# Attention and two feed-forward layers in float32: the first 24 attention steps and the first block of both layers as whole float32 products, and the weights split after that block has used them

## The chip, the cores and the metric

The kernel runs on one core of one Trainium2 chip. The core has a matrix engine (TensorE, "PE" in the profile, with its weight loads shown apart as "PEld"), three engines that work on vectors (VectorE "DVE", ScalarE "ACT", GpSimd "POOL"), and SyncE ("SP"), from which this kernel issues all its DMAs. The engines run side by side, each through its own instructions in order, and wait for each other through semaphores. The metric is the device time of one execution in microseconds, lower is better.

## The reference

```python
# 8 batches, 8 heads, 512 local and 32 global tokens, head size 64; float32
s_g = scale * np.matmul(q_g, k_all.transpose(0, 1, 3, 2))
out_g = np.matmul(sm(s_g), v_all)                  # 32 global queries see all 544 keys
s_ll = np.where(np.abs(pos[:, None] - pos[None, :]) <= 32, s_ll, -1e9)
a_l = sm(np.concatenate([s_lg, s_ll], axis=-1))    # a local query: the 32 global keys and a window of 65
out_l = np.matmul(a_l, np.concatenate([v_g, v_l], axis=2))
...
x = attn_out.transpose(0, 2, 1, 3).reshape(4352, 512)
h = x @ w_in                                       # 512 x 2048
g = h * (1.0 / (1.0 + np.exp(-h)))
return (g @ w_out).astype(np.float32)              # 2048 x 512
```

The weights come as float64; the kernel turns them into float32 on the chip.

## The kernel before

**Products of split operands.** PE takes operands of the type float32r, which hold fewer bits than float32. To keep float32 accuracy, nearly every operand is split: ACT writes a rounded copy "hi" (a CAST), and DVE or POOL writes the rest "lo" as a difference. One wanted product is then three on PE: hi by hi, hi by lo, lo by hi. So the queries and keys of a step become qk and klo (`st_split`, L339/L340 for the first 28 steps, L342 to L344 later), the values vhi and vlo (L350/L351), the transposed probabilities pt_hi and pt_lo (L396/L397, and for the columns of the global queries L404/L405), the attention output xh and xl (L427/L428), the activations gh and gl (L559/L560), and the weights w_hi and w_lo (L238/L239).

**Attention in steps.** A step is a chunk of 128 local queries for a pair of heads; there are 128 steps, 16 to a batch. Step k loads its queries and keys (`st_load`), splits them, forms the scores (`st_scores`, L369: 6 products of 224 columns), runs the softmax on DVE and ACT (L373 to L382), and copies the probabilities by a DMA from SBUF to SBUF into a float32r tile rr (L385), since the transposes take float32r. `st_turn` transposes four 128x128 blocks on PE (L393) and splits the result; `st_out` multiplies by the values (L421: 12 products of 128 or 160 columns, for 64 output rows) and writes 128 rows of the layers' input. The global queries of a batch go the same way in four pairs of heads: `g_load`, `g_split` (L253 to L255), `g_scores` (L268 to L270: 6 products of 272 columns), `g_soft`, `g_move` (two DMAs to float32r tiles rg), `g_turn` (10 transposes a batch, L310/L313).

**Weights.** `load_weights` brings in one piece of a slice: 512 columns (256 towards the end) of 128 rows as pairs of 32-bit words. ACT scales the upper words (L231), three integer operations of DVE put the float32 together (L233, L234, L236), ACT casts w_hi (L238) and POOL subtracts w_lo (L239). There are 16 slices f, each with 512 columns of the first layer's weights and 512 of the second's.

**The two layers in blocks.** The token tiles (128 rows each) are taken in 12 blocks of three or two (`SIZES`). For each block and each slice f, `first_layer` issues 12 products of 384 columns (L550), the activation follows (tanh on ACT L556, DVE L557, then the split), and `second_layer` of the slice before issues 9 products of 512 columns (L569 to L571).

**Order.** PE's program order is the order in which the Python code emits it; the other engines' instructions are put in order by a scheduler at build time. The attention is a list of pieces with due times (`DUE`, `LAG`, `HEADS`), and `advance` emits those that are due. Before block 0 the code emits steps 0 to 11, which feed block 0's three token tiles; during block n the call `fill` emits the steps that block n+1 needs, so steps 12 to 23 run beside block 0. During block 0 each slice also asks for the weights three slices ahead (`LOOK`). Buffers that only the first steps use live in two pools (`first_pool`) that are closed once they are empty and whose room then holds the last four slices of weights.

Of the kernel before, what the change touches and what calls it, by code (L numbers as in the profile page):

```python
# [33 lines left out]
NEG = -8.0e9              # times the scale of 1/8: -1e9  # L34
SCALE = 0.125

# [1 line left out]
SIZES = [3, 2] + [3] * 9 + [2]       # token tiles in each block of the two layers  # L38
NLATE = 4                            # slices of the weights that take the place of the first buffers
# [19 lines left out]
PRE, PACE, LOOK = 0, 0.75, 1         # weights converted during the first steps  # L59
END = 0.6                            # how far the attention is ahead of a block  # L60
# [13 lines left out]
CLOSE = 9  # L74
# [16 lines left out]
ND = 28  # L91

@with_exitstack
def attention_moe_kernel(ctx: ExitStack, tc: tile.TileContext, qk0_in, qk_in, v_in, gqk, wts, out):
# [7 lines left out]
    # buffers of the first steps, in two parts that later hold the last slices of the weights  # L102
# [6 lines left out]
    # until the layers start, attention has their banks too  # L109
# [33 lines left out]
    # probabilities: columns past the window stay zero  # L143
    probs = []
    for i in range(BUFS["p"]):
        t = const.tile([P, 2, 2 * P], F32, name=f"probs{i}")
# [5 lines left out]
    held = [set() for _ in first]  # L152
    pts = []
    for home in (const, first_pool[0])[: 1 + (PTS > 0)]:
        pts.append([home.tile([P, 2, 2, P + SG], F32R, name=f"pt_{part}{len(pts)}") for part in ("hi", "lo")])
        for t in pts[-1]:
            nc.gpsimd.memset(t.bitcast(F32), 0.0)
    if PTS:
        held[0].add(f"pt{PTS - 1}")

    def pt_tiles(k):
        return pts[k % 2 if k < PTS else 0]
# [4 lines left out]
    closing, turns, uses = [], itertools.count(), itertools.count()  # L167
# [5 lines left out]
    def raw_tile(name):  # L173
        if first[0] and not closing and next(uses) % 3 == 0:
            held[0].add(name)
            return first_pool[0].tile([P, QW + KW], F32, tag="raw", name=name)
        return raws.tile([P, QW + KW], F32, tag="raw", name=name)

    def qk_tiles(name):
        if first[0] and not closing and next(turns) % 3 == 0:  # L180
            held[0].add(name)
            pool, bufs = first_pool[0], (1, 1)
        else:
            pool, bufs = work, BUFS["qk"]
        return (pool.tile([P, QW + KW], F32R, tag="qk", bufs=bufs[0], name=f"qk{name}"),
                pool.tile([P, SKV], F32R, tag="klo", bufs=bufs[1], name=f"klo{name}"))

    def rr_tile(k):
        if k % 2 and k < RRS and first[0]:
            held[0].add(f"rr{k}")  # L190
            return first_pool[0].tile([P, 4 * P], F32R, tag="rr", bufs=1, name=f"rr{k}")
        return work.tile([P, 4 * P], F32R, tag="rr", bufs=BUFS["rr"], name=f"rr{k}")
# [4 lines left out]
    w_hi, w_lo, w_next = [], [], [0, 0]  # L197

    def load_weights():
        f, c0 = w_next  # L200
        i = (f - (NF - NLATE)) // 2
        if f == CLOSE and not closing:
            closing.append(f)
        if i >= 0 and first[i]:
# [5 lines left out]
            first_pool[i] = ctx.enter_context(tc.tile_pool(name=f"late{i}", bufs=1, side=side, reuse_waits="tile"))  # L210
        if c0 == 0:
            home = const if i < 0 else first_pool[i]
            w_hi.append(home.tile([P, 2 * DM], F32R, name=f"w_hi{f}"))
            w_lo.append(home.tile([P, 2 * DM], F32R, name=f"w_lo{f}"))
# [13 lines left out]
        # float64 to float32: the upper word read as float32 and scaled by 2**-112 has the exponent  # L228
# [439 lines left out]
```

## Time and profile before

| what | value |
|---|---|
| time, median of 3 runs (lowest, highest) | 1109.2 us (1108.95, 1109.77) |
| span of the profiled execution | 1108.1 us |
| time of a run beyond that span, by the median | 1.1 us |
| first product of the first layer, block 0 | 86.37 us |
| first product of the first layer, block 1 | 206.58 us |
| bytes moved by DMA | 134.76 MB, of them 86.44 MB read from HBM |

Times inside the execution count from the start of its span. "Busy" is the time in which an engine has an instruction in work; on PE successive products overlap, so what one product costs is read from the distance between the starts of two neighbours, not from its duration. The row PEclk gives the share of full speed at which TensorE's clock was granted. A form such as `128x384 f32` is partitions by elements.

### The profile page before, as it was taken

The page shows a single profiled execution, that of the slowest core. Times are in us where ns is not written, and L with a number is a line of the kernel's source. Part 1 is how long each engine was busy: PE and PEld are TensorE (multiplying, and loading weights), DVE is VectorE, ACT ScalarE, POOL GpSimd, SP SyncE. Part 2 cuts the span into 40 slices and gives each one's busy share as a digit, 9 for nine tenths or more (in the row PEclk, how much of TensorE's full clock was granted, in tenths as well). Part 3 has the DMA queues.
Part 4 walks back from the last instruction along what each step waited for, and adds up shares of the span by engine and source line. Part 5 has one row for each costly group of instructions (what it writes and reads, how often), then busy time and mean ns, then how long its engine had stood idle before and what let it go on. Part 6 is the DMA issues. An engine that isn't in the chain of part 4 may idle for free.

```text
span 1108.1 us, 21579 instructions
## 1 busy us (share of the span) xinstructions
PE 1042.5 (94%) x6824; PEld 947.8 (86%) x6824; DVE 798.5 (72%) x2467; ACT 725.1 (65%) x1933; POOL 228.5 (21%) x441
## 2 busy tenths in 40 slices
PE   5647889999999999999999999999999999999998
PEld 4646778898999999999989999999999999889996
DVE  6989998777778867766667877777777768863322
ACT  7876676776677766766567776667666658763232
POOL 8756775321100111001010111101100011100000
PEclk8678899999999999999999999999999999999999
DMA  8576554543343443342233443334333324420000
GB/s 249 179 219 188 182 170 130 156 121 117 109 145 115 138 138 110 113 148 83 82 112 112 147 130 117 111 116 158 109 109 120 111 92 148 138 76 20 1 30 19
DMA packets 74800, 134.76 MB, mean 122 GB/s; under 512 B 10432, under 2 KB 30400, under 8 KB 74688
## 3 DMA queue, kind: packets, MB, share of 16 engines
q1 hardware_dynamic: 74688, 133.40, 38.8%
q8 instruction: 54, 0.88, 0.3%
q14 instruction: 58, 0.48, 0.1%
HBM read 86.44 MB, written 8.91 MB: 86 GB/s over the span
## 4 chain that ended last, share of the span: by engine, by line
PE 80%; DVE 10%; DMA 3%; issue 3%; ACT 3%; POOL 1%; SPq 0%; DVEq 0%; ACTq 0%; POOLq 0%
PE h L550 31%; PE out L569 11%; PE out L571 10%; PE out L570 10%; PE o L421 8%; PE s L369 4%; PE t L393 3%; DVE w L234 2%; DVE w L236 1%; DMA rr<-probs 1%; DMA raw_w<-in_wts_dram 1%; DVE raw_w L233 1%; DVE pt_lo L397 1%; ACT probs L377 1%; DVE probs L373 1%
## 5 line engine op out<-in xcount | busy, mean ns | idle before, releaser
L550 PE MATMUL h<-xh,w_hi 128*128 128x384 f32 (+1 forms) x768 | 255.6, 333 | 0.1
L550 PE MATMUL h<-xh,w_lo 128*128 128x384 f32 (+1 forms) x768 | 252.3, 329 | 0.0
L550 PE MATMUL h<-xl,w_hi 128*128 128x384 f32 (+1 forms) x768 | 252.1, 328 | 0.0
L569 PE MATMUL out<-w_hi,gh 128*128 128x512 f32 x544 | 224.8, 413 | 0.0
L571 PE MATMUL out<-w_hi,gl 128*128 128x512 f32 x544 | 215.6, 396 | 3.0 <-DVE gl L560 1.8
L570 PE MATMUL out<-w_lo,gh 128*128 128x512 f32 x544 | 214.7, 395 | 0.0
L556 ACT ACTIVATE t<-h 128x384 f32<-128x384 f32 (+1 forms) x192 | 90.5, 471 | 186.2 <-PE h L550 175.8
L404 POOL CAST pt_hi<-pgt 128x64 fp32r<-128x64 f32 (+1 forms) x160 | 50.4, 327 | 726.1 <-PE o L421 719.2
L557 DVE SCALAR_TENSOR_TENSOR t<-t,h 128x384 f32<-128x384 f32 (+1 forms) x192 | 101.6, 529 | 122.7 <-ACT t L556 121.7
L550 PEld LDWEIGHTS h<-xh,w_hi 128*128 128x128 f32 x768 | 145.4, 189 | 6.0 <-ACT xh L427 0.6
L550 PEld LDWEIGHTS h<-xl,w_hi 128*128 128x128 f32 x768 | 145.5, 189 | 5.4
L550 PEld LDWEIGHTS h<-xh,w_lo 128*128 128x128 f32 x768 | 145.3, 189 | 0.0
L560 DVE TENSOR_TENSOR gl<-t,gh 128x384 fp32r<-128x384 f32 (+1 forms) x192 | 107.3, 559 | 48.5 <-PE out L571 43.1
L571 PEld LDWEIGHTS out<-w_hi,gl 128*128 128x128 f32 x544 | 102.8, 189 | 28.4 <-DVE gl L560 4.6
L377 ACT ACTIVATE probs<-probs,st 128x224 f32<-128x224 f32 x256 | 121.4, 475 | 7.3 <-DVE st L373 6.2
L373 DVE CUSTOM_DVE_ANT_0 probs<-s,mask 128x224 f32<-128x224 f32 x256 | 89.3, 384 | 50.4 <-PE s L369 47.0
L421 PE MATMUL o<-pt_hi,vhi 128*64 128x160 f32 (+1 forms) x512 | 99.4, 238 | 20.1 <-ACT pt_hi L396 7.8
L570 PEld LDWEIGHTS out<-w_lo,gh 128*128 128x128 f32 x544 | 103.6, 190 | 11.2
L569 PEld LDWEIGHTS out<-w_hi,gh 128*128 128x128 f32 x544 | 103.2, 190 | 11.4 <-ACT gh L559 0.4
L559 ACT CAST gh<-t 128x384 fp32r<-128x384 f32 (+1 forms) x192 | 94.6, 493 | 21.2 <-DVE t L557 17.8
L421 PE MATMUL o<-pt_hi,vlo 128*64 128x160 f32 (+1 forms) x512 | 96.3, 237 | 0.0
L421 PE MATMUL o<-pt_lo,vhi 128*64 128x160 f32 (+1 forms) x512 | 79.8, 238 | 16.3 <-DVE pt_lo L397 11.8
(82 smaller groups left out, 2016.5 us busy)
## 6 DMA issues: line engine op xcount, KB each, us to landing
raw<-in_qk_dram SPq DMA_DIRECT2D x100, 352.0 KB, 3.0
rr<-probs SPq DMA_DIRECT2D x128, 256.0 KB, 2.3
vraw<-in_v_dram SPq DMA_DIRECT2D x128, 128.0 KB, 2.4
raw_w<-in_wts_dram SPq DMA_DIRECT2D x28, 512.0 KB, 4.0
raw_g<-in_gqk_dram SPq DMA_DIRECT2D x32, 304.0 KB, 2.8
out_dram<-o SPq DMA_DIRECT2D x32, 256.0 KB, 2.6
raw<-in_qk_dram SPq DMA_DIRECT2D x28, 240.0 KB, 3.6
rg<-pg SPq DMA_DIRECT2D x16, 256.0 KB, 2.4
```

The lines of the kernel that those rows point to most:

```text
L373: nc.vector.tensor_tensor_reduce(out=p[:, u, :W], in0=s[:, u * W : (u + 1) * W], in1=mask_of[c], scale=-SCALE, scalar=3.0e38, op0=ALU.add, ...
L377: nc.scalar.activation(p[:, u, :W], p[:, u, :W], AF.Exp, bias=st[:, u : u + 1], scale=-1.0, accum_out=st[:, 2 + u : 3 + u])
L404: nc.gpsimd.tensor_copy(out=pt_hi[:n, :, a, P:], in_=g)
L421: nc.tensor.matmul(o[:D, u * wide : u * wide + m], v[:, a, u, :], pt[:, u, a, :m], start=(i == 0), stop=(i == len(terms) - 1))
L550: nc.tensor.matmul(h[:, :nt], wt, x[:, c, :nt], start=(i == 0), stop=(i == 3 * NCC - 1))
L556: nc.scalar.activation(t[:, :nt], h[:, :nt], AF.Tanh, scale=0.5)
L557: nc.vector.scalar_tensor_tensor(out=t[:, :nt], in0=t[:, :nt], scalar=1.0, in1=h[:, :nt], op0=ALU.add, op1=ALU.mult)
L559: nc.scalar.copy(out=gh[:, :nt], in_=t[:, :nt])
L560: nc.vector.tensor_tensor(out=gl[:, :nt], in0=t[:, :nt], in1=gh[:, :nt].bitcast(F32), op=ALU.subtract)
L569: nc.tensor.matmul(o, gh[:, sl], wh, start=(f == 0), stop=False)
L570: nc.tensor.matmul(o, gh[:, sl], wl, start=False, stop=False)
L571: nc.tensor.matmul(o, gl[:, sl], wh, start=False, stop=(f == NF - 1))
```

## The change

- For the first 24 steps (`KF`) and the global queries of the first two batches (`GF`) nothing is split. Scores, transposes and value products take the float32 tiles as they were loaded: a product is one instruction with float32 operands where three with float32r stood. The copies rr and rg are not made for them; the transposes read the probabilities themselves.
- Block 0's input, activations and weights stay float32 too: 4 products instead of 12 in `first_layer`, 3 instead of 9 in `second_layer`. Half of the copies of block 0's input move from ACT to DVE; its xl and gl are not made.
- `load_weights` makes only the float32 weights, with two DVE operations instead of three; ACT's scaling uses the function Prelu with a slope instead of Copy. `split_weights(f)`, called behind block 0's `second_layer` of slice f, makes w_hi on ACT and w_lo on POOL for the later blocks. The float32 slice f lies where w_lo of slice f+1 will lie, and the last one lies in the buffer of block 0's xl.
- Buffers: five tiles of probabilities instead of two in the first 12 steps, up to six for the loaded queries and keys, two single tiles for transposed probabilities where one hi/lo pair stood. The first weight pools are closed one slice earlier, and `CLOSE` goes from 9 to 8.

```diff
+KF = 24
+GF = 2
-CLOSE = 9
+CLOSE = 8
...
-        nc.scalar.activation(w, words[:, :, 1].bitcast(F32), AF.Copy, scale=2.0**-112)
-        wi, up, low = w.bitcast(U32), words[:, :, 1].bitcast(U32), words[:, :, 0].bitcast(U32)
-        nc.vector.tensor_scalar(out=up, in0=wi, scalar1=3, scalar2=None, op0=ALU.logical_shift_left)
-        nc.vector.scalar_tensor_tensor(out=wi, in0=wi, scalar=0x80000000, in1=up, op0=ALU.bitwise_and,
+        nc.scalar.activation(w, words[:, :, 1].bitcast(F32), AF.Prelu, scale=2.0**-112, alpha=-(2.0**32))
+        wi, low = w.bitcast(U32), words[:, :, 0].bitcast(U32)
+        nc.vector.tensor_scalar(out=low, in0=low, scalar1=29, scalar2=None, op0=ALU.logical_shift_right)
+        nc.vector.scalar_tensor_tensor(out=wi, in0=wi, scalar=3, in1=low, op0=ALU.logical_shift_left,
                                        op1=ALU.bitwise_or)
-        nc.vector.scalar_tensor_tensor(out=wi, in0=low, scalar=29, in1=wi, op0=ALU.logical_shift_right,
-                                       op1=ALU.bitwise_or)
-        nc.scalar.copy(out=hi, in_=w)
-        lows(2 * f + c0 // DM < POOLW).tensor_tensor(out=lo, in0=w, in1=hi.bitcast(F32), op=ALU.subtract)
+    def split_weights(f):
+        w_hi.append(slot(f, late, F32R, "wh", f"w_hi{f}"))
+        w_lo.append(slot(f, late, F32R, "ws", f"w_lo{f}"))
+        for c0 in range(0, 2 * DM, DM):
+            sl = slice(c0, c0 + DM)
+            hi, lo, w = w_hi[f][:, sl], w_lo[f][:, sl], w_32[f][:, sl]
+            nc.scalar.copy(out=hi, in_=w)
+            nc.gpsimd.tensor_tensor(out=lo, in0=w, in1=hi.bitcast(F32), op=ALU.subtract)
...
     def st_scores(k, b, c, pr):
-            if k < ND:
+            if k < KF:
+                terms = [(raw[:, qs], raw[:, QW : QW + W])]
+            elif k < ND:
...
     def st_turn(k, b, c, pr):
+            if whole:
+                nc.tensor.transpose(t[:, i * P : (i + 1) * P], p[:, i * P : (i + 1) * P], ident.bitcast(F32))
+                continue
             nc.tensor.transpose(t[:, i * P : (i + 1) * P].bitcast(F32R), rr[:, i * P : (i + 1) * P], ident)
...
     def st_out(k, b, c, pr, t):
+            if whole:
+                terms = [(vraw, pt_f, a) for a in range(2)]
...
-            nc.scalar.copy(out=xh[rows, pr, sl], in_=src)
-            nc.vector.tensor_tensor(out=xl[rows, pr, sl], in0=src, in1=xh[rows, pr, sl].bitcast(F32),
-                                    op=ALU.subtract)
+            if n == 0 and u == 0:
+                nc.scalar.copy(out=xh[rows, pr, sl], in_=src)
+            elif n == 0:
+                nc.vector.tensor_copy(out=xh[rows, pr, sl], in_=src)
...
     def first_layer(n, f):
+            if n == 0:
+                nc.tensor.matmul(h[:, :nt], w_32[f][:, c * P : (c + 1) * P], xh[:, c, :nt], start=(c == 0),
+                                 stop=(c == NCC - 1))
+                continue
...
     def second_layer(n, f, gh, gl):
+            if n == 0:
+                nc.tensor.matmul(o, gh[:, sl], wh, start=(f == 0), stop=(f == NF - 1))
...
+        if n == 0:
+            split_weights(f)
```

More of the change, by code (lines that the diff above doesn't have):

```diff
@@ L91 @@
 ND = 28
+KF = 24
+GF = 2
+RRS = 12
 @with_exitstack
@@ L144, in attention_moe_kernel @@
     probs = []
-    for i in range(BUFS["p"]):
-        t = const.tile([P, 2, 2 * P], F32, name=f"probs{i}")
+    for i in range(BUFS["p"] + 3):
+        home = const if i < BUFS["p"] else first_pool[0]
+        t = home.tile([P, 2, 2 * P], F32, name=f"probs{i}")
         nc.gpsimd.memset(t, 0.0)
@@ L152, in attention_moe_kernel, with pt_whole, probs_tile @@
     held = [set() for _ in first]
+    held[0].update(f"p{k}" for k in range(RRS) if k % len(probs) >= BUFS["p"])
     pts = []
[L154 to L159, printed above, removed]
-    def pt_tiles(k):
-        return pts[k % 2 if k < PTS else 0]
+    def pt_tiles(k):
+        if not pts:
+            for part in ("hi", "lo"):
+                pts.append(work.tile([P, 2, 2, P + SG], F32R, tag=f"pt_{part}", name=f"pt_{part}"))
+                nc.gpsimd.memset(pts[-1].bitcast(F32), 0.0)
+        return pts
+    def pt_whole(k):
+        return work.tile([P, 2, 2, P + SG], F32, tag="pt_lo" if k % 2 else "pt_hi", name=f"pt{k}")
+    def probs_tile(k):
+        i = k % (len(probs) if k < RRS else BUFS["p"])
+        held_by[i] = k
+        return probs[i]
+    held_by = {}
     acc = const.tile([P, NPR, P], F32, name="acc")
-    closing, turns, uses = [], itertools.count(), itertools.count()
+    closing, homes = [], itertools.count()
     def free(name):
@@ L171, in free, with raw_tile @@
             names.discard(name)
-    def raw_tile(name):
-        if first[0] and not closing and next(uses) % 3 == 0:
+    def raw_tile(name, whole=False):
+        i = next(homes) % (2 if closing else 3) if whole else 0
+        if i == 2:
             held[0].add(name)
-            return first_pool[0].tile([P, QW + KW], F32, tag="raw", name=name)
+            return first_pool[0].tile([P, QW + KW], F32, tag="raw", bufs=2, name=name)
+        if i == 1:
+            return work.tile([P, QW + KW], F32, tag="qk", bufs=BUFS["qk"][0], name=name)
         return raws.tile([P, QW + KW], F32, tag="raw", name=name)
     def qk_tiles(name):
[L180 to L186, printed above, removed]
+        return (work.tile([P, QW + KW], F32R, tag="qk", bufs=BUFS["qk"][0], name=f"qk{name}"),
+                work.tile([P, SKV], F32R, tag="klo", bufs=BUFS["qk"][1], name=f"klo{name}"))
     def rr_tile(k):
-        if k % 2 and k < RRS and first[0]:
-            held[0].add(f"rr{k}")
-            return first_pool[0].tile([P, 4 * P], F32R, tag="rr", bufs=1, name=f"rr{k}")
         return work.tile([P, 4 * P], F32R, tag="rr", bufs=BUFS["rr"], name=f"rr{k}")
@@ L195, in lows, with slot @@
         return nc.gpsimd if pool else nc.vector
-    w_hi, w_lo, w_next = [], [], [0, 0]
+    w_32, w_hi, w_lo, w_next = [], [], [], [0, 0]
+    def slot(i, late, dtype, tag, name):
+        home = const if i < NF - NLATE else first_pool[(i - (NF - NLATE)) // 2]
+        assert i < NF - NLATE or late[(i - (NF - NLATE)) // 2]
+        return home.tile([P, 2 * DM], dtype, tag=f"{tag}{i}", name=name)
+    late = [False, False]
     def load_weights():
         f, c0 = w_next
-        i = (f - (NF - NLATE)) // 2
+        i = (f + 1 - (NF - NLATE)) // 2
         if f == CLOSE and not closing:
             closing.append(f)
-        if i >= 0 and first[i]:
+        if 0 <= i < 2 and first[i]:
             while held[i]:
@@ L327, in st_vload @@
     def st_vload(k, b, c, pr):
-        vraw = raws.tile([P, 2, 2, D], F32, tag="vraw", bufs=BUFS["vraw"], name=f"vraw{k}")
+        if k < KF and k % 2:
+            vraw = two.tile([P, 2, 2, D], F32, tag="vhi" if k % 4 == 1 else "vlo", name=f"vraw{k}")
+        else:
+            vraw = raws.tile([P, 2, 2, D], F32, tag="vraw", bufs=BUFS["vraw"], name=f"vraw{k}")
         nc.sync.dma_start(out=vraw.rearrange("p a u d -> p (a u d)"), in_=v_in[b, c, pr])
@@ L355, in st_scores @@
     def st_scores(k, b, c, pr):
-        qk, klo = tiles.pop(("qk", k))
-        free(k)
+        if k < KF:
+            raw = tiles.pop(("raw", k))
+            free(f"raw{k}")
+        else:
+            qk, klo = tiles.pop(("qk", k))
+            free(k)
         s = attbank("s", f"s{k}")
@@ L411, in st_out @@
         sl = slice(i * P, (i + 1) * P)
-        vhi, vlo = tiles.pop(("v", k))
-        pt_hi, pt_lo = pt_tiles(k)
+        whole = k < KF
+        if whole:
+            vraw, pt_f = tiles.pop(("vraw", k)), tiles.pop(("pt", k))
+        else:
+            vhi, vlo = tiles.pop(("v", k))
+            pt_hi, pt_lo = pt_tiles(k)
         free(f"pt{k}")
@@ L417, in st_out @@
         for u in range(2):
-            terms = [(v, pt_hi, a) for a in range(2) for v in (vhi, vlo)] + [(vhi, pt_lo, a) for a in range(2)]
+            if whole:
+                terms = [(vraw, pt_f, a) for a in range(2)]
+            else:
+                terms = [(v, pt_hi, a) for a in range(2) for v in (vhi, vlo)] + [(vhi, pt_lo, a) for a in range(2)]
             for i, (v, pt, a) in enumerate(terms):
```

113 lines of the change are left out of this document (79 added, 34 removed).

## Prediction

> **What bounds the kernel now.** I read the page first: the busy shares and the slices tell whether one engine bounds the whole.
>
> ```profile
> PE 1042.5 (94%) x6824; PEld 947.8 (86%) x6824; DVE 798.5 (72%) x2467; ACT 725.1 (65%) x1933; POOL 228.5 (21%) x441
> ...
> PE   5647889999999999999999999999999999999998
> ...
> PEclk8678899999999999999999999999999999999999
> ```
>
> PE is busy 94% of the span, but not evenly: nine tenths and more from the seventh slice on, 4 to 8 before, with a clock granted at 6 to 8 tenths in the first four slices. So I cut the span where PE's work changes: at the first product h of block 0 and of block 1, by PE's timeline (start, duration, what).
>
> ```profile
> 86.37 0.55 PE L550 MATMUL h<-xh,w_hi 128*128 128x384 f32 x1
> ...
> 206.58 0.34 PE L550 MATMUL h<-xh,w_hi 128*128 128x384 f32 x1
> ```
>
> The windows view, cut there and at the starts of blocks 2 and 3, gives for each stretch the length, then the busy time of each engine, the granted clock, the share of the DMA engines and GB/s.
>
> ```profile
> core 0: us, PE busy (x) PEld busy (x) DVE busy (x) ACT busy (x) POOL busy (x), PEclk, DMA share, GB/s
> 0.00:86.40 86.40, 48.68 (x329) 43.51 (x329) 69.43 (x203) 66.86 (x181) 61.85 (x89) 0.74 0.70 216
> 86.40:206.60 120.20, 101.75 (x615) 89.26 (x615) 110.84 (x274) 85.51 (x223) 74.22 (x85) 0.93 0.54 162
> 206.60:300.40 93.80, 91.71 (x614) 83.23 (x613) 69.25 (x223) 65.67 (x175) 19.48 (x40) 1.00 0.42 127
> 300.40:391.30 90.90, 90.87 (x611) 83.26 (x610) 70.64 (x231) 64.85 (x175) 9.73 (x32) 1.00 0.43 132
> 391.30:1108.00 716.70, 709.50 (x4662) 648.57 (x4660) 478.35 (x1538) 442.21 (x1182) 63.22 (x196) 1.00 0.33 101
> ```
>
> Call the stretches A (86.4 us, steps 0 to 11), B (120.2 us, block 0 with steps 12 to 23 beside it) and C (the 901.5 us from 206.6 to the end at 1108.1). In C, PE is busy 91.71 of 93.80, 90.87 of 90.90 and 709.50 of 716.70 us at clock 1.00: PE alone bounds it. In B it is not PE (101.75 of 120.20) but DVE with 110.84. In A nothing is full: DVE 69.43 of 86.40, ACT 66.86, POOL 61.85, DMA 0.70, PE 48.68 at a clock of 0.74. The chain of waits over the first 215 us names the same engine:
>
> ```profile
> by line: DVE w L234 11.5%; issue 10.7%; DVE w L236 7.1%; DMA raw_w<-in_wts_dram 5.5%; DVE raw_w L233 5.0%; PE h L550 4.9%; ACT probs L377 4.0%; DVE pt_lo L397 3.7%; PE o L421 3.4%; DVE probs L373 2.4%; DVE probs L382 2.3%; POOL klo L340 2.3
> ```
>
> The largest parts are DVE's three operations on weights (L234, L236, L233: 23.6% together). The reader should keep one thing: A and B hold the slack, C has none, and what the change does not move in A or B it does not move at all.
>
> **The price of a PE product.** From the timeline of PE at full clock, the distances of starts:
>
> ```profile
> 217.87 0.34 PE L550 MATMUL h<-xh,w_hi 128*128 128x384 f32 x1
> ...
> 219.98 0.23 PE L421 MATMUL o<-pt_hi,vhi 128*64 128x160 f32 x1
> ...
> 220.78 0.32 PE L369 MATMUL s<-qk 128*128 128x224 f32 x1
> ...
> 221.50 0.40 PE L569 MATMUL out<-w_hi,gh 128*128 128x512 f32 x1
> ...
> 223.57 0.46 PE L393 MATMUL t<-ident,rr 128*128 128x128 f32 x4
> 223.87 0.41 PE L550 MATMUL h<-xh,w_hi 128*128 128x384 f32 x1
> ...
> 226.03 0.28 PE L268 MATMUL gs<-qk_g 128*64 128x272 f32 x1
> ...
> 226.76 0.39 PE L569 MATMUL out<-w_hi,gh 128*128 128x512 f32 x1
> ```
>
> Twelve products h of 384 columns take 219.98 - 217.87 = 2.11 us, 0.176 each; twelve products o take 0.80, 0.067 each; six scores 0.72, 0.120 each; nine products out 2.07, 0.230 each; four transposes 0.30, 0.075 each; six products gs 0.73, 0.122 each.
>
> No row shows a product with float32 operands. Lower bound: one float32r product (0.176 for h). Upper bound: four that do not overlap at all, at the 0.34 us that one lasts, 1.36. I take four at the distance of their starts, 0.70: the three that stood there leave out lo by lo, and a product that leaves nothing out has four such parts; of all rows this is the nearest. In the Trainium skill, FP8 and Floating Point Precision, TensorE Precision Notes, true FP32 is four passes through the array, H*H, H*L, L*H and L*L; no run here shows it yet, and the sum by that page would be the one below. A transpose of float32 has the same two bounds in kind, one float32r transpose (0.075) or four (0.30); I take one, because the row of the same move of the same tile is the nearest and a transpose has no parts to add, and I keep four as a rival.
>
> **Stretch A, part by part.** How much PE work lies in A:
>
> ```profile
> L369 PE MATMUL s<-qk 128*128 128x224 f32 x28 | 11.1, 396 | 0.0
> ...
> L268 PE MATMUL gs<-qk_g 128*64 128x272 f32 x14 | 5.0, 360 | 4.5 <-ACT qk_g L253 4.5
> ```
>
> 28 products of each kind are 14 steps of scores, 14 are 7 pairs of global heads; the turns and value products are those of 12 steps. After the change, at full clock: scores 14 x 2 x 4 x 0.120 = 13.4; values 12 x 4 x 4 x 0.067 = 12.9; transposes 12 x 0.30 = 3.6; global scores 7 x 2 x 4 x 0.122 = 6.8; global transposes 10 x 0.075 = 0.8. Sum 37.5 us, against 29.2 by the same rows for three products. At A's granted clock of 0.74 that is 50.7.
>
> The other engines lose work:
>
> ```profile
> L234 DVE SCALAR_TENSOR_TENSOR w<-w,raw_w 128x512 uint32<-128x512 uint32 x10 | 11.5, 1148 | 0.2
> ...
> L397 DVE TENSOR_TENSOR pt_lo<-t,pt_hi 128x512 fp32r<-128x512 f32 x12 | 8.1, 677 | 0.4 <-ACT pt_hi L396 0.3
> L236 DVE SCALAR_TENSOR_TENSOR w<-raw_w,w 128x512 uint32<-128x512 uint32 x9 | 7.8, 862 | 0.2
> L233 DVE TENSOR_SCALAR raw_w<-w 128x512 uint32<-128x512 uint32 x10 | 7.7, 766 | 4.5 <-ACT w L231 4.5
> L428 DVE TENSOR_TENSOR xl<-o,xh 64x128 fp32r<-64x128 f32 x22 | 6.1, 279 | 0.5
> L254 DVE TENSOR_TENSOR klo_g<-raw_g,qk_g 128x544 fp32r<-128x544 f32 x8 | 5.9, 742 | 3.8 <-ACT qk_g L253 3.8
> ```
>
> DVE loses pt_lo 8.1, klo_g 5.9, xl 6.1 (twelve copies of some 0.28, 3.4, come back) and one of three weight operations. I take away L234, 11.5, and keep the other two at their present price, since each of the two that stay is of one of these kinds. 69.4 - 8.1 - 5.9 - 6.1 + 3.4 - 11.5 = 41.2.
>
> ```profile
> L339 ACT CAST qk<-raw 128x480 fp32r<-128x480 f32 x15 | 8.8, 585 | 1.3 <-POOL pt_hi L404 0.8 <-DMA raw<-in_qk_dram 0.5
> ...
> L238 ACT CAST w_hi<-w 128x512 fp32r<-128x512 f32 x9 | 5.6, 618 | 1.5 <-DVE w L236 1.5
> ```
>
> ACT loses the casts qk 8.8 now and w_hi 5.6 to B, and vhi and qk_g beside them: 52.5 at most, of 66.9.
>
> ```profile
> L340 POOL TENSOR_TENSOR klo<-raw,qk 128x480 fp32r<-128x480 f32 x15 | 18.9, 1261 | 11.4 <-ACT qk L339 10.0 <-PE gs L269 1.4
> L239 POOL TENSOR_TENSOR w_lo<-w,w_hi 128x512 fp32r<-128x512 f32 x9 | 12.2, 1357 | 1.2 <-ACT w_hi L238 1.1
> L351 POOL TENSOR_TENSOR vlo<-vraw,vhi 128x256 fp32r<-128x256 f32 x13 | 11.3, 871 | 1.1 <-ACT vhi L350 1.0
> ```
>
> POOL loses 18.9 + 11.3, and 12.2 goes to B: 19.5 is left of 61.9.
>
> ```profile
> DMA packets 9776, 18.68 MB, mean 216 GB/s; under 512 B 1337, under 2 KB 5416, under 8 KB 9768
> ...
> rr<-probs SPq DMA_DIRECT2D x12, 256.0 KB, 3.0
> ```
>
> The copies rr, 12 x 256 KB = 3.1 of 18.68 MB, go; DMA is 0.70 x 86.4 = 60.5 us of full load, and 50.5 after. They leave SP's queue too, so no load waits behind a copy that waits for a softmax.
>
> So the busiest in A are PE with 50.7 and DMA with 50.5. A now takes 86.4 / 69.4 = 1.245 times its busiest engine (start-up, waits from step to step). With the same ratio A becomes 1.245 x 50.7 = **63 us**: 23 saved. What ends last there next is PE, no longer DVE.
>
> **Stretch B.** PE after: h 64 x 4 x 0.176 = 45.1 (33.8 now); out 48 x 4 x 0.230 = 44.2 (33.1 now); twelve steps of 0.96 + 1.07 + 0.30, 28.0 (21.8 now); two pairs of global scores 1.9 and ten transposes 0.8. Sum **120.0**, against 91.0 now by the same rows. The other engines come under it:
>
> ```profile
> L234 DVE SCALAR_TENSOR_TENSOR w<-w,raw_w 128x512 uint32<-128x512 uint32 x19 | 20.6, 1085 | 0.4
> ...
> L560 DVE TENSOR_TENSOR gl<-t,gh 128x384 fp32r<-128x384 f32 x15 | 12.8, 854 | 0.0
> ...
> L397 DVE TENSOR_TENSOR pt_lo<-t,pt_hi 128x512 fp32r<-128x512 f32 x12 | 8.2, 680 | 0.0
> ```
>
> DVE's 110.8 falls by gl 12.8, pt_lo 8.2 and one weight operation, 20.6, to 69. POOL has 74.2, to which at most 12.2 of late splits come. The splits of w_hi and w_lo are thus hidden by PE's 120; each needs only to be done before block 1, and if that cover were gone the last slice's two subtractions of 1.36 alone would cost some 3 us. The clock in B is 0.93 now and I take 1.00, since PE no longer stands still. PE-bound stretches take 1.00 times PE (block 2) and B today takes 120.2 / 110.8 = 1.085 times its DVE; I take 1.03 between them: **123.6 us**, 3.4 more than now. B is no gain: one bound takes the place of another.
>
> **Sum.** 63 + 123.6 + 901.5 = 1088.1 of span, against 1108.1. The median of the runs is 1.1 us above the profiled span, so 1089.
>
> **The rivals.**
>
> 1. *Float32 products are cheaper than four.* At three parts, PE in B falls by a quarter of the 115 us of products to about 91, and ACT's present 85.5 x 1.085 = 93 is beside it. B 93, A 60: about 1056. For it: only bounds are known. Against it: the missing fourth part.
>
> 2. *Transposes cost four times theirs.* B gains 12 x 0.90 + 2.3 = 13 and becomes 137; A's PE becomes 50 us, 54 at B's clock of 0.93, so A is 67: 63 + 4 and 123.6 + 13.4 give 1107. At the clock of 0.74 A stays near 84 and it is slower than before.
>
> 3. *A is not shortened much, because loads or the chain from step to step hold it.* The changed A has no room left in DMA if the weights are fetched ahead into the time that becomes free. With A at 80, 1106.
>
> 4. *Slower: the weight load of a float32 product stands on PE's path.*
>
> ```profile
> L550 PEld LDWEIGHTS h<-xh,w_hi 128*128 128x128 f32 x768 | 145.4, 189 | 6.0 <-ACT xh L427 0.6
> ```
>
> A load lasts 189 ns and is hidden now, since the matmul before it covers it. Were a load of 0.189 bare ahead of each float32 product, B would gain (64 + 48 + 12 x 10) x 0.189 = 44 and A's PE 26. With half of them bare: 1089 + 35 = 1124. It decides from about a third: then the 20 saved are gone. Against it: fewer products means fewer loads, and a longer product covers one better. The Trainium skill, TensorE: Matmul & The Clock Gate, Weight-path perf modes, says that the fast weight load is off for FP32; that is this rival's mechanism, and no run here shows it.
>
> 5. *Prelu is not in the loaded table set.*
>
> ```profile
> L253 ACT ACT_TABLE_LOAD x1 | 1.3, 1283 | 0.7 <-PEq L657 0.7
> ```
>
> There is one table load now, 1.28 us. If Prelu needs another set than Exp and Tanh, each of 36 pieces brings two: 92 us of ACT. A's ACT would be 52 + 31 = 83, times 1.245 is 103, B's 85 + 62 = 147, times 1.085 is 160; total about 1165, less where pieces follow each other without an Exp between. The Trainium skill, ScalarE: Activation LUTs, Table sets, says that cheap functions (relu, copy, abs) stand in every set; Prelu is not in its list, and no run here shows it.
>
> **How the numbers follow.** Forecast 0.55 (1079 to 1100, by A from 58 to 70 and B from 118 to 129); rival 1 0.08; rival 2 0.15; rival 3 0.10; rival 4 0.08; rival 5 0.04. Range 1070 to 1112: it takes in the forecast, rivals 2 and 3 but for their ends, and leaves out rivals 1, 4 and 5, 0.20. About 0.2% (2.2 us) is what a measurement of this kernel can tell from no change. Faster: 0.55 + 0.08 + half of rival 2 + 0.7 of rival 3 = 0.78, of which I keep 0.77; the same 0.05; slower 0.18.
>
> **What would show it.** Right: starts of float32 products h 0.70 us apart (or four parts of 0.176); transposes in four at 0.30; block 0 beginning near 63 us; B with PE busy at nine tenths and DVE near 70 us; one table load; C within 3 us of 901.5. Wrong: B below 110 (rival 1), turns of 1.2 us (2), DMA above 0.8 in A with block 0 beginning at 80 (3), PEld waits in front of each product (4), many table loads (5). Most doubtful is the price of a float32 product: each tenth of a part is 2.9 us in B.

## The result and the profile after

The changed kernel takes 1089.4 us (median of 4 runs, 1088.31 to 1090.38) against 1109.5 us before: a ratio of 0.9819, 95% interval 0.9805 to 0.9833. The forecast was 1089. Its profiled execution spans 1088.5 us. Of all executions of the experiments below one, of the kernel "layers split again, 3 operations", was slow, with 2031.9 us; the ratio there leaves it out, and the median of the other three is 1086.8 and not 1087.3. The page of the profile of the changed kernel, with the same rows as before:

```profile
PE 1054.8 (97%) x6552; PEld 918.4 (84%) x6552; DVE 727.4 (67%) x2367; ACT 690.0 (63%) x1847; POOL 156.8 (14%) x368
...
PE   6799979999999999999999999999999999999998
...
PEclk9989998999999999999999999999999999999999
```

PE reaches nine tenths in the third slice now instead of the seventh, and the clock is granted at 8 to 9 tenths from the start, where it was 6 to 8. The windows view, cut as in the prediction (first h of block 0, of block 1, starts of blocks 2 and 3):

```profile
core 0: us, PE busy (x) PEld busy (x) DVE busy (x) ACT busy (x) POOL busy (x), PEclk, DMA share, GB/s
0.00:62.90 62.90, 46.32 (x239) 34.53 (x240) 37.76 (x157) 47.17 (x135) 15.86 (x46) 0.92 0.79 261
62.90:189.40 126.50, 116.14 (x434) 69.01 (x433) 72.04 (x219) 70.29 (x183) 47.56 (x54) 0.97 0.37 114
189.40:284.20 94.80, 92.71 (x612) 82.89 (x611) 68.95 (x223) 65.69 (x175) 20.58 (x42) 1.00 0.40 124
284.20:375.20 91.00, 90.98 (x612) 83.34 (x611) 70.46 (x231) 64.88 (x175) 9.72 (x32) 1.00 0.42 132
375.20:1088.50 713.30, 708.67 (x4662) 648.61 (x4660) 478.17 (x1538) 441.97 (x1182) 63.09 (x196) 1.00 0.33 102
```

| stretch | before | forecast | after |
|---|---|---|---|
| A, steps 0 to 11 | 86.4 | 63 | 62.9 |
| B, block 0 | 120.2 | 123.6 | 126.5 |
| C, the rest | 901.5 | 901.5 | 899.1 |

A gives 23.5 us, B takes 6.3 back, and C gives 2.4. In B the time is not all PE's: it is busy for 116.1 of 126.5 us, so it stands still for 10.4. DVE, with 110.8 us the fullest engine of B before, has 72.0.

**The prices on PE.** The chain of waits in B (start, duration, what) shows the new products one behind the other without a gap:

```profile
74.92 0.76 PE s L418 x4
75.68 2.58 PE h L634 x8
78.26 0.44 PE t L452 x4
78.69 2.58 PE out L663 x6
```

Each product with float32 operands shows as two rows of the trace, so "h x8" is the 4 products that `first_layer` issues for a slice. One product h of 384 columns is 2.58 / 4 = 0.645 us, that is 0.645 / 0.176 = 3.67 float32r products; a product out is 2.58 / 3 = 0.86, and a step's scores, two products of 224 columns, are 0.76. The transposes are 0.44 for four, where float32r ones took 0.30. The clock was granted at 1.00 here, as it was where the prediction took its prices.

**Where A's time went.** The view of waits on PE in A, first of the kernel before (what stood, what it waited for: us in total, times, longest; "issue" is time in which it waited for nothing that the profile shows):

```profile
PE o L421 <- DVE pt_lo L397: 7.5, 8, 2.1
PE o L421 <- DVE acc L435: 6.9, 1, 6.9
PE o L421 <- ACT pt_hi L396: 5.8, 5, 1.4
PE gt L310 <- DMA rg<-pg: 5.4, 1, 5.4
PE gs L268 <- ACT qk_g L253: 4.5, 2, 4.3
PE o L421 <- DVE st L379: 3.9, 2, 2.6
```

then of the kernel after:

```profile
PE o L498 <- issue: 4.8, 3, 2.7
PE o L498 <- ACT pt L460: 4.2, 2, 2.6
PE gs L296 <- DMA raw_g<-in_gqk_dram: 3.9, 1, 3.9
PE gt L346 <- DVE pg L320: 3.1, 2, 1.5
```

PE stood for 86.40 - 48.68 = 37.7 us and stands for 62.90 - 46.32 = 16.6, so 21.1 of the 23.5 us are waits and 2.4 is busy time. The waits for the split pt and the copy rg (pt_lo, pt_hi, rg: 18.7 us) are gone; what stands there now is smaller, 4.2 us for the copy pt among it. The longest single stand of before, 6.9 us, is put down to acc, the sum for the global queries on DVE, and is of another kind. The chain of waits over A leads from that acc back through DVE's and ACT's order to a piece of weights:

```profile
57.47 7.73 DMA raw_w<-in_wts_dram
```

ACT stood for 3.23 us until this piece landed, then scaled it, and the softmax and acc came behind. No stand of this length is left in A. The wait of 4.3 us for qk_g at the start was mostly for a load; as a load it is still there, 3.9.

**Where B's new time is.** PE's two longest stands in B, by its timeline, are before two groups of value products (in brackets the idle time and its releaser):

```profile
150.47 1.17 PE L498 MATMUL o<-pt,vraw 128*64 128x160 f32 x8 [3.54 <-ACT pt L460]
...
164.20 2.15 PE L498 MATMUL o<-pt,vraw 128*64 128x160 f32 x8 [4.42 <-DVE qk_g L278]
```

The chain of waits over 145 to 166 us says what released them; its pieces in order of time:

```profile
142.59 2.93 DMA raw_w<-in_wts_dram
...
145.54 0.45 ACT w L247
...
146.01 0.43 DVE w L250
...
146.46 2.98 DMA raw_w<-in_wts_dram
...
150.39 3.49 DMA raw_w<-in_wts_dram
```

This is a loop: a piece of weights lands, ACT scales it, DVE finishes it, and at the end of that operation (146.01 + 0.43 = 146.44) the DMA of the next piece starts (146.46), into the buffer that has just come free. A turn takes 3.9 us, nearly 3 of them a transfer. Nothing in the loop belongs to PE. ACT's timeline shows how it reaches PE all the same:

```profile
145.54 0.44 ACT L247 ACTIVATE w<-raw_w 128x256 f32<-128x256 f32 x1 [3.44 <-DMA raw_w<-in_wts_dram]
...
149.47 0.44 ACT L247 ACTIVATE w<-raw_w 128x256 f32<-128x256 f32 x1 [1.10 <-DMA raw_w<-in_wts_dram]
149.81 0.56 ACT L460 COPY pt<-t 128x512 f32<-128x512 f32 x1
...
153.90 0.44 ACT L247 ACTIVATE w<-raw_w 128x256 f32<-128x256 f32 x1 [3.53 <-DMA raw_w<-in_wts_dram]
...
161.37 0.62 ACT L259 CAST w_hi<-w 128x512 fp32r<-128x512 f32 x1 [0.47 <-DVE w L250]
162.53 0.70 ACT L276 CAST qk_g<-raw_g 128x608 fp32r<-128x608 f32 x1 [0.55 <-DMA raw_g<-in_gqk_dram]
163.14 0.48 ACT L646 ACTIVATE t<-h 128x384 f32<-128x384 f32 x1
163.52 0.58 ACT L460 COPY pt<-t 128x512 f32<-128x512 f32 x1
```

ACT runs in order. The transposes before the first stand were issued on PE at 142.14. Their copy (L460) stands behind the scaling of two pieces (L247), for whose transfers ACT stood 3.44 and 1.10 us, and begins only at 149.81. The next value product on PE, which reads pt, begins at 150.47, behind the copy. Before the second stand the transposes were issued at 155.97 (by PE's timeline, a group of four of 0.60), but their copy begins only at 163.52, behind pieces, a softmax, w_hi and qk_g, and ends at 164.10; the product that reads it begins at 164.20. The profile puts this wait down to qk_g L278, which merely ended last before it; the product doesn't read that tile. Between these transposes and their copy ACT itself stood for only 1.5 us; the rest is work that came ahead of the copy. So in the second stand the pieces are a part, and how large a part is not shown.

### The profile page after: what moved, and what is told of

Its sections match the earlier page's. It is cut to its first block, busy times and chain, and to the rows that moved or that the text cites. A ratio compares the mean times of both kernels' runs of the same rounds, so it can differ in the third digit from the quotient of the medians.

```text
span 1088.5 us, 20485 instructions
## 1 busy us (share of the span) xinstructions
PE 1054.8 (97%) x6552; PEld 918.4 (84%) x6552; DVE 727.4 (67%) x2367; ACT 690.0 (63%) x1847; POOL 156.8 (14%) x368
## 4 chain that ended last, share of the span: by engine, by line
PE 93%; DMA 3%; DVE 2%; ACT 1%; issue 1%; SPq 0%; DVEq 0%
PE h L640 32%; PE out L665 11%; PE out L667 10%; PE out L666 10%; PE o L498 10%; PE s L418 6%; PE out L663 3%; PE h L634 3%; PE t L454 3%; DMA raw_w<-in_wts_dram 3%; PE gs L296 1%; PE t L452 1%; PE gs L298 1%; PE gs L300 1%; PE gs L299 1%
## 5 line engine op out<-in xcount | busy, mean ns | idle before, releaser
L640 PE MATMUL h<-xh,w_hi 128*128 128x384 f32 (+1 forms) x704 | 232.6, 330 | 0.0
L640 PE MATMUL h<-xh,w_lo 128*128 128x384 f32 (+1 forms) x704 | 229.8, 326 | 0.0
L640 PE MATMUL h<-xl,w_hi 128*128 128x384 f32 (+1 forms) x704 | 229.6, 326 | 0.0
L665 PE MATMUL out<-w_hi,gh 128*128 128x512 f32 x496 | 203.7, 411 | 0.0
L667 PE MATMUL out<-w_hi,gl 128*128 128x512 f32 x496 | 195.3, 394 | 0.0
L666 PE MATMUL out<-w_lo,gh 128*128 128x512 f32 x496 | 194.5, 392 | 0.0
L648 DVE SCALAR_TENSOR_TENSOR t<-t,h 128x384 f32<-128x384 f32 (+1 forms) x176 | 92.9, 528 | 124.1 <-ACT t L646 123.3
L640 PEld LDWEIGHTS h<-xl,w_hi 128*128 128x128 f32 x704 | 132.6, 188 | 5.3 <-issue 0.2
L426 ACT ACTIVATE probs<-probs,st 128x224 f32<-128x224 f32 x256 | 121.3, 475 | 12.7 <-DVE st L422 11.8
L652 ACT CAST gh<-t 128x384 fp32r<-128x384 f32 (+1 forms) x176 | 86.5, 491 | 20.0 <-DVE t L648 16.6
L430 ACT ACTIVATE probs<-probs,st 128x224 f32<-128x224 f32 x128 | 61.7, 482 | 43.7 <-DVE st L429 40.8
L383 ACT CAST qk<-raw 128x704 fp32r<-128x704 f32 x100 | 78.1, 781 | 15.3 <-PE s L418 14.8
L509 ACT CAST xh<-o 64x128 fp32r<-64x128 f32 x232 | 59.5, 257 | 40.6 <-PE o L498 28.3
```

The source lines that it names most:

```text
L383: nc.scalar.copy(out=qk, in_=raw)
L426: nc.scalar.activation(p[:, u, :W], p[:, u, :W], AF.Exp, bias=st[:, u : u + 1], scale=-1.0, accum_out=st[:, 2 + u : 3 + u])
L640: nc.tensor.matmul(h[:, :nt], wt, x[:, c, :nt], start=(i == 0), stop=(i == 3 * NCC - 1))
L648: nc.vector.scalar_tensor_tensor(out=out[:, :nt], in0=t[:, :nt], scalar=1.0, in1=h[:, :nt], op0=ALU.add, op1=ALU.mult)
L652: nc.scalar.copy(out=gh[:, :nt], in_=t[:, :nt])
L665: nc.tensor.matmul(o, gh[:, sl], wh, start=(f == 0), stop=False)
```

## The experiments

Each time is a median beside runs of the kernel before on the same chip; A, B and C are those of one profiled execution, whose time can lie some us from the median (up to 6 in the run with the layers split and 12 whole steps). The kernel before took 1108.3 to 1109.9 us on the chips of these runs, so rows of different chips compare to some 1.5 us. Except where said, an edit is against the changed kernel.

| kernel | us | ratio to before, 95% | A | B | C |
|---|---|---|---|---|---|
| before | 1109.5 | 1 | 86.4 | 120.2 | 901.6 |
| after | 1089.4 | 0.9819 (0.9805 to 0.9833) | 62.9 | 126.5 | 899.1 |
| attention split again | 1129.0 | 1.0175 (1.0152 to 1.0197) | 82.4 | 145.7 | 900.5 |
| layers split again, 3 operations | 1087.3 | 0.9800 (0.9780 to 0.9819) | 61.5 | 123.7 | 899.9 |
| 3 operations on weights | 1095.8 | 0.9878 (0.9860 to 0.9896) | 65.9 | 129.7 | 900.5 |
| CLOSE 5 | 1088.8 | 0.9821 (0.9806 to 0.9835) | 61.9 | 125.9 | 899.1 |
| late pieces in other buffers | 1088.5 | 0.9818 (0.9796 to 0.9840) | 60.4 | 123.3 | 901.3 |
| layers split again, 2 operations | **1081.9** | 0.9762 (0.9740 to 0.9784) | 63.1 | 119.6 | 898.2 |
| copies rr again | 1103.3 | 0.9950 (0.9934 to 0.9965) | 75.2 | 128.9 | 900.9 |
| KF 28 | 1091.8 | 0.9840 (0.9820 to 0.9861) | 63.2 | 127.9 | 900.9 |
| before, 2 operations | 1115.0 | 1.0060 (1.0043 to 1.0076) | 86.3 | 124.6 | 902.9 |
| queries and keys split again | 1113.0 | 1.0045 (1.0030 to 1.0060) | 71.6 | 137.4 | 901.1 |
| layers split, 12 whole steps | 1089.1 | 0.9837 (0.9808 to 0.9867) | 64.5 | 128.4 | 900.2 |
| values split again | 1099.5 | 0.9929 (0.9912 to 0.9945) | 74.4 | 122.4 | 899.4 |

### Which half of the change pays

**The attention split again**, block 0 left whole:

```diff
-KF = 24
-GF = 2
+KF = 0
+GF = 0
...
-    for i in range(BUFS["p"] + 3):
+    for i in range(BUFS["p"]):
```

and the buffers for raw, qk, klo and rr as before the change.

> Attention split as before in all steps (with the buffers of before), block 0, weights and late splits as in the changed kernel. My theory (A is shortened mainly because the whole steps take work off DVE, ACT, POOL and DMA): stretch A goes back most of the way, to 75 to 82 us of 86.4 (only the third weight operation and the splits of weights are gone from it), B is near 118, the time 1093 to 1105. Rival (the lighter handling of weights and block 0 carry the gain): A 65 or less, time 1092 or less.

It took 1129.0 us: 39.6 more than after, 24 above what was expected, and slower than before. A went back to 82.4 as expected; B was missed by 28. Its windows:

```profile
0.00:82.40 82.40, 49.95 (x328) 45.55 (x329) 60.36 (x189) 65.43 (x171) 49.34 (x82) 0.71 0.76 242
82.40:228.20 145.80, 119.46 (x507) 71.74 (x505) 85.44 (x229) 77.28 (x203) 71.52 (x87) 0.89 0.40 126
```

In B, PE is busy for 119.5 us and stands for 26.3. So the whole attention steps do not only shorten A, they also take waits out of B.

**The layers split again**, attention left whole: block 0 and the weights as before the change, with the three operations.

```diff
+NB = 0
...
+            w_hi.append(slot(f, late, F32R, "wh", f"w_hi{f}"))
+            w_lo.append(slot(f, late, F32R, "ws", f"w_lo{f}"))
...
+        nc.scalar.copy(out=hi, in_=w)
+        lows(2 * f + c0 // DM < POOLW).tensor_tensor(out=lo, in0=w, in1=hi.bitcast(F32), op=ALU.subtract)
...
-            if n == 0:
+            if n < NB:
```

> Steps 0 to 23 whole, but block 0 and the weights as before the change (three weight operations, hi and lo at once, 12 and 9 products). My theory (B is bound by PE, and whole products cost PE more than three): PE's work in B falls by 17 us to some 99, DVE's rises by about 28 to 100; A 66 to 72; B 105 to 115; the time 1075 to 1090, so no slower than the changed kernel. Rival (block 0 has to be whole, since DVE bounds B otherwise): B 120 or more, time 1095 or more.

1087.3 us: the time is within what was expected and 2.1 less than after, but its parts are not. A is 61.5 and not 66 to 72, and B is 123.7, where the rival had it, and not 105 to 115. The attention alone brings the whole gain. In its B, DVE is busy again for 100.5 us:

```profile
61.50:185.20 123.70, 106.95 (x546) 90.34 (x545) 100.47 (x266) 80.43 (x207) 50.08 (x55) 0.93 0.45 133
```

**The same with the two operations** of the change; the diff is against the kernel just above, whose other two DVE lines come back with it:

```diff
 NB = 0
-        nc.scalar.activation(w, words[:, :, 1].bitcast(F32), AF.Copy, scale=2.0**-112)
+        nc.scalar.activation(w, words[:, :, 1].bitcast(F32), AF.Prelu, scale=2.0**-112, alpha=-(2.0**32))
```

> As e2_lay_split (steps 0 to 23 whole; block 0 split, weights split at once), but with the change's two weight operations. Theory (B of e2 is held by DVE, 100.9 of 123.7 us, since PE has only 107 there): DVE falls to some 87 in B, B to 108 to 116, A to 59 to 61, the time to 1069 to 1079, clearly under the changed kernel, so whole products in block 0 are a loss once the conversions are short. Rival (late weights hold B in both, whatever the products are): B 120 or more, time 1082 or more.

1081.9 us, the fastest of all. It lies between the two expectations, at the rival's edge.

```profile
63.10:182.60 119.50, 105.61 (x545) 89.85 (x544) 77.38 (x233) 78.35 (x205) 43.36 (x52) 0.93 0.43 129
```

Against after, PE is busy 116.14 - 105.61 = 10.5 us less in B, and B is 7 us shorter. So with whole attention steps the whole block 0, with the late splits that go with it, costs 1089.4 - 1081.9 = 7.5 us.

### The conversion of the weights

**Three operations in the changed kernel:**

```diff
-        nc.scalar.activation(w, words[:, :, 1].bitcast(F32), AF.Prelu, scale=2.0**-112, alpha=-(2.0**32))
+        nc.scalar.activation(w, words[:, :, 1].bitcast(F32), AF.Copy, scale=2.0**-112)
```

with the three DVE operations of before behind it.

> The changed kernel with the three weight operations of before (and Copy instead of Prelu). My theory (DVE bounds neither A nor B any more: 37.8 of 62.9 and 72.0 of 126.5 us): DVE gains some 25 us, the time stays within 4 us of the changed kernel, 1088 to 1093. Rival (the dropped operation was on the path, since weights are late in B): 1096 or more.

1095.8 us, 6.4 more than after; this lies nearer to the rival. A and B are some 3 us longer each.

**Two operations in the kernel before**, nothing else changed there. This one asks whether relieving DVE alone shortens A and B:

```diff
-        nc.scalar.activation(w, words[:, :, 1].bitcast(F32), AF.Copy, scale=2.0**-112)
+        nc.scalar.activation(w, words[:, :, 1].bitcast(F32), AF.Prelu, scale=2.0**-112, alpha=-(2.0**32))
```

> The kernel before with nothing changed but the weights' conversion: two DVE operations instead of three, Prelu instead of Copy. It closes a square: attention whole or split, block 0 whole or split, all with two operations. My theory (DVE holds A and B of the kernel before): some 9 us come off DVE in A and 20 in B, A 80 to 84, B 108 to 116, time 1096 to 1104; against e6_lay_conv2 the whole steps are then worth 14 to 22 us. Rival (the conversions alone make most of the gain): 1092 or less.

```profile
0.00:86.30 86.30, 51.33 (x329) 45.65 (x330) 64.29 (x198) 68.90 (x183) 60.67 (x90) 0.69 0.69 223
86.30:210.90 124.60, 102.76 (x615) 91.25 (x615) 98.60 (x242) 84.00 (x220) 68.95 (x85) 0.90 0.48 153
```

A miss. DVE lost 69.43 - 64.29 = 5.1 us in A and 110.84 - 98.60 = 12.2 in B, yet A stayed at 86.3, B grew by 4.4, and the time rose to 1115.0, 6.7 above the kernel before on the same chip. So less work on DVE alone shortens neither stretch. That DVE stood off the path does not follow: in the chain of waits over B its operations on weights fell from 28.5% to 14.7%, but transfers of weights rose from 3.4% to 19.7% and took their place. Why they came to the path was not settled; the scheduler at build time orders the other engines anew for every variant, so single effects of some 5 us in this table are not to be put down to one operation.

### The late pieces

**The first weight pools closed earlier:**

```diff
-CLOSE = 8
+CLOSE = 5
```

> The changed kernel with CLOSE 5 instead of 8: the first steps' buffers stop being used earlier, so that the pool from which the late slices of weights get their room is empty earlier. Theory (the 10 us in which PE stands in B come from weights that are late, because between 83 and 109 us no piece could be brought in): the gap in the conversions shrinks, B goes from 126.5 to 117 to 123, time 1080 to 1086. Rival (PE's stands in B come from the order of the steps, or the small pieces' two buffers set the pace): B 126, time 1088 to 1091.

1088.8 us, no difference from after, so the rival held. Slices 11 and 12 were converted at 86 to 90 us instead of 110, but the small pieces still began at 131.

**The late pieces in two buffers of another pool:**

```diff
-            raw = raws.tile([P, QW + KW], I32, tag="raw", name=f"raw_w{f}_{c0}")[:, : 2 * n]
+            raw = two.tile([P, DM], I32, tag="o", name=f"raw_w{f}_{c0}")[:, : 2 * n]
```

> The changed kernel; the twelve small pieces of weights at the end land in two buffers of their own (the pair that later stages the output, idle until block 0 ends) instead of the pair that the steps' loads also use. Theory (PE's 10 us of standing in B come from slices 13 to 15 being late, whose pieces wait for a buffer that a step holds until its scores, and then follow each other every 4 us): conversions of the last twelve pieces begin before 115 us, B falls from 126.5 to 116 to 120, the time to 1079 to 1084. Rival (the stands come from the order of the steps in B): B 126, time 1088 to 1090.

1088.5 us: missed. The conversions of the small pieces began at 112.7 us, as expected, and the last began at 141.5 instead of 175, but the time stayed. In ACT's timeline the same order is to be seen:

```profile
140.74 0.43 ACT L247 ACTIVATE w<-raw_w 128x256 f32<-128x256 f32 x1 [2.47 <-DMA raw_w<-in_wts_dram]
141.19 0.26 ACT L509 CAST xh<-o 64x128 fp32r<-64x128 f32 x1
141.48 0.43 ACT L247 ACTIVATE w<-raw_w 128x256 f32<-128x256 f32 x1
141.81 0.57 ACT L460 COPY pt<-t 128x512 f32<-128x512 f32 x1
```

and the row of PE behind it:

```profile
142.48 0.76 PE L498 MATMUL o<-pt,vraw 128*64 128x160 f32 x2 [5.43 <-ACT pt L460]
```

The stand of 3.5 us became one of 5.4 at another place. More buffers move the loop; they don't take the pieces out of ACT's order. In B PE stands for 8.4 us here (123.3 less 114.95), 2.0 less than after.

### Which part of a whole step pays

For these, KF is taken apart into KQ (queries and keys), KT (probabilities into the transposes) and KV (transposed probabilities and values). **The copies rr (through one buffer) and float32r transposes again in the first 24 steps:**

```diff
-KF = 24
+KQ, KT, KV = 24, 0, 24
```

> The changed kernel with the copies of the probabilities and the float32r transposes of before in steps 0 to 23 (one buffer for the copy); scores and values stay whole. Theory (A is carried by all four relieved engines, the DMA among them: 49.7 us of full load of 62.9): 3 MB more in A put DMA to some 58 us of load and add 2 to 4 us of waiting to each turn, A 68 to 76; transposes in four fall from 0.44 to 0.30; time 1093 to 1103. Rival (only the splits on the engines mattered, a copy is hidden): A 65 or less, time 1091 or less.

1103.3 us, at the edge of what was expected. A is 75.2, and the waits on PE in A name the copy:

```profile
PE t L456 <- DMA rr<-probs: 15.2, 7, 5.2
```

**Queries and keys split again:**

```diff
-KF = 24
+KQ, KT, KV = 0, 24, 24
```

> The changed kernel with the queries and keys of steps 0 to 23 split as before (cast on ACT 0.59 us, difference on POOL 1.3 us a step, products of three); transposes and values stay whole, no copies are made. Theory (A is held by a chain through loads, PE and the softmax, and no single engine; DMA load matters most): ACT gets 7 us and POOL 16 us more in A, both still under 55; PE does 12 x 0.1 less; A 63 to 69, time 1089 to 1096. Rival (the splits on ACT and POOL were what held A): A 72 or more, time 1098 or more.

1113.0 us: the rival held. A is 71.6 and B 137.4; the splits cost 8.7 us in A. POOL waits there for ACT's casts, and PE for both, though for no more than 6.1 us:

```profile
POOL klo L381 <- ACT qk L380: 20.1, 10, 4.0
```

```profile
PE s L418 <- POOL klo L381: 3.2, 3, 1.5
PE s L418 <- ACT qk L380: 2.9, 3, 1.5
```

The larger loss is B's, 10.9 us. There PE's longest waits are for ACT's copy pt, 9.7 us where after had 3.5; that ACT comes to it later because of the casts is likely, but not shown.

```profile
PE o L500 <- ACT pt L462: 9.7, 4, 3.7
```

**Values and transposed probabilities split again:**

```diff
-KF = 24
+KQ, KT, KV = 24, 24, 0
```

> The changed kernel with the values and the transposed probabilities of steps 0 to 23 split as before; scores and transposes stay whole, no copies are made. Theory (the parts of the whole steps add up in A: splitting everything gives 82.4, that is 19.5 more than the changed kernel, of which the copies are 12.3 and the split of queries and keys 8.7): nothing is left for the values, A 62 to 66; PE in B does 12 x 0.32 = 3.8 less, ACT 12 x 0.4, DVE 12 x 0.68 and POOL 12 x 1.3 more; B 123 to 130, time 1087 to 1096. Rival (the parts do not add up, any split on POOL and DVE holds A): A 69 or more, time 1098 or more.

1099.5 us, the rival again. A is 74.4, and PE stands before the value products for both halves of the split:

```profile
PE o L500 <- DVE pt_lo L466: 8.7, 9, 3.3
PE o L500 <- ACT pt_hi L465: 7.1, 6, 3.0
```

Put back one at a time, the three parts cost A 12.3, 8.7 and 11.6 us, 32.6 together, while all three at once (with the global queries) cost 19.5. So these are not three terms of a sum but, most likely, links of one chain from step to step: any one of them puts back much of what all together did. Part of the excess may be buffers: the kernel with all three has those of before for raw, qk, klo and rr, while the copies alone went through one buffer.

### How many steps

**Four steps more:**

```diff
-KF = 24
+KF = 28
```

> The changed kernel with 28 whole steps instead of 24: steps 24 to 27 stand at the end of B and in the first part of C, where PE alone bounds the time. Theory (a whole step costs PE 0.5 to 0.6 us more than a split one, by 0.86 + 1.12 + 0.44 against 0.67 + 0.80 + 0.30, and relieving the other engines is worth nothing where PE is full): 4 x 0.55 = 2.2 us slower than the changed kernel, 1090 to 1093. Rival (relief of DVE and ACT is still worth something there): 1089 or less.

1091.8 us, as expected: those steps fall at the end of B and behind it, where PE stands still no more, and there a whole step costs PE time. The 2.4 us are near the edge of what these runs can tell.

**Only the first 12**, in the fastest kernel:

```diff
-KF = 24
+KF = 12
```

> As e6_lay_conv2, but with only the first 12 steps whole; steps 12 to 23, beside block 0, are split as before. Theory (whole steps pay where PE has room, that is in A; in B each costs PE 0.55 us more but takes some 1.5 us off DVE, 1 us off ACT, 3 us off POOL): PE in B 105.7 - 6.6 = 99, DVE 77.7 + 12 = 90, ACT 92, POOL 85; B within 4 us of e6's 119.6, time 1078 to 1086. Rival (in B too the relief is what counts): B 125 or more, time 1088 or more.

1089.1 us, 7.2 more than with 24; the rival held. Its profiled execution took 1095.2, so the gain is read from the medians: steps 12 to 23, beside block 0, gain about 7 us by being whole. PE is busy for as long in B either way (105.2 us against 105.6), but split at a granted clock of 0.89 and whole at 0.93; DVE is busy for 102.3 us split and for 77.4 whole.

## Why the prediction was right, and where not

The time was right; the sum reached it with two errors that nearly cancel (B 2.9 us too low, C 2.4 too high), and one of its steps fell.

- **A, 63 us: the number held, its reason did not, and that it fell so close is in part luck.** The step that failed is the rule that A takes 1.245 times its busiest engine, which reads DVE's 69.4 of 86.4 us as what set A. With 5.1 us less DVE work in A, the kernel before kept A at 86.3. And no engine is full in A after: DMA 0.79, ACT 47.17 and PE 46.32 of 62.90 us. PE's 50.7 was too high, with the clock granted at 0.92 and not 0.74; by the same rule PE's measured 46.3 gives 57.7 and the DMA's 49.7 gives 61.9. DMA (0.79 x 62.9 = 49.7 against 50.5) and ACT (47.2 against at most 52.5) came as worked out. That PE ends last next, and no longer DVE, held: in the chain of waits over A after, PE's own products (o, gs, s, t) are 52.7%, where before DVE's three operations on weights had 21.3% and PE's largest part, o, 3.3%.

```profile
by line: PE o L498 19.5%; PE gs L296 13.8%; PE s L418 10.4%; DMA raw_w<-in_wts_dram 9.9%; issue 9.6%; PE t L452 9.0%; DMA raw_g<-in_gqk_dram 4.9%; DVE raw_w L249 4.0%; ACT w L247 3.5%; DVE probs L422 3.0%; ACT w_hi L259 2.1%; DVE w L250 1.9
```

What the runs showed in place of the rule is the chain from step to step: PE's waits for splits and copies, each of which put back costs A 8.7 to 12.3 us. The view of waits on PE in A had 18.7 us of them for pt_lo, pt_hi and rg alone, and 6.9 behind a piece of weights. It names where the time would come from; it does not give the sum, since other waits grew.

- **B, 123.6 us: right in kind, short in size.** That PE takes DVE's place as the fullest engine held (116.1 us; DVE 72.0 against 69). Two terms were off. PE's work is 116.1 and not 120.0: scores, h and out came cheaper than four parts (0.76 against 0.96 a step, 0.645 against 0.70, 0.86 against 0.92), transposes and values dearer (0.44 against 0.30 a step, 1.1 to 1.2 against 1.07). And the allowance for PE's stands was 3.6 us where 10.4 came. Its two largest, 7.9 us together, lie in ACT's order, the first behind pieces of weights, the second behind pieces and other work; the prediction called the late splits "hidden by PE's 120" and did not ask what stands behind the late work on ACT. Nor was DVE the only bound of B before: with 12.2 us less of it B grew.
- **C within 3 us of 901.5:** held, 899.1. Over all kernels C lies between 898.2 and 902.9; the 2.4 us were not looked into.
- **Rival 1, cheaper than four products:** h is 3.67 parts and not 3, so it held by a third, and PE stayed the fullest engine. The Trainium skill, FP8 and Floating Point Precision, TensorE Precision Notes, gives four passes for true FP32; the trace has h 8% below four float32r products, in two rows a product.
- **Rival 2, transposes at four times:** false; 0.44 / 0.30 = 1.47.
- **Rival 3, A held by loads at 80:** false; 62.9 at a DMA share of 0.79. The chain from step to step that it names besides loads is real, but the change shortened it.
- **Rival 4, slower by bare weight loads:** false. In the chain above, products follow each other without a gap, though each load lasts as long as before:

```profile
L634 PEld LDWEIGHTS h<-x,w 128*128 128x128 f32 x127 | 24.1, 193 | 17.5 <-issue 5.1
```

- **Rival 5, table loads:** false; the one that there was is the only one:

```profile
L301 ACT ACT_TABLE_LOAD x1 | 1.3, 1283 | 0.7 <-PEq L755 0.7
```

What the change is made of, by the medians: the two operations alone took the kernel before from 1109.5 to 1115.0; whole attention on top brought it to 1081.9 (33.1 less); whole block 0 on top brought it to 1089.4 (7.5 more). In the other order, the whole block costs 14.0 (1115.0 to 1129.0) and whole attention then gains 39.6. By either order the attention is the gain and the whole block a loss. The two operations hang on the attention as well: with split steps they cost time, with whole ones they gain 6.4 us (1095.8 to 1089.4) or, with the layers split, 5.4 (1087.3 to 1081.9); each of these is near the size that a new order of the other engines may make alone.

**Open:** what sets B in full. In after, the two largest stands are shown, by the order on ACT and, for the first, the loop of pieces. In the fastest kernel PE still stands for 13.9 us in B (119.5 less 105.6); transfers of weights are 20.5% of the chain of waits there, but what each stand waits for was not followed. No kernel was made in which the pieces leave ACT's order, so that their share is shown by the traces alone and not by taking it away.

## What to carry to other kernels

Where no engine is full, look for a saving in what the late engine waits for and not in the busiest engine's sum: the waits on PE named splits and copies in A, and taking 17 us from the busiest DVE gained nothing as long as the attention was split. Trading three cheap products and their splits for one dear product pays where PE waits for the splits, and costs where PE is full, as in block 0's layers. Before calling late background work hidden, look at what stands behind it in the order of its engine: here a piece that waited some 3 us for its transfer held up the copy for TensorE queued behind it.

## What the runs showed of the hardware

- A product with float32 operands shows as two rows on PE and costs 3.67 float32r products at 384 columns (0.645 against 0.176 us) and 3.74 at 512 (0.86 against 0.230). The ratio is not the same for all shapes: the scores, of 224 columns, cost 0.38 / 0.120 = 3.17.
- Four float32 transposes of 128x128 take 0.44 us against 0.30 for float32r, both at clock 1.00: 1.47 times, not four.
- A's clock was granted at 0.89 to 0.97 in the kernels whose first 12 steps are whole (0.92 in after), at 0.82 to 0.86 in the three where one part of a step was put back, and at 0.69 to 0.74 in the three that split all of them there (before, before with two operations, and after with the attention split). What the clock follows was not tried.
